# The front of an FNet-plus-MLP kernel: 128-column warm products, ScalarE centering part of the fourth chunk, first products ahead of the last transposes, and w1's second chunk in 4 loads

## The chip, the cores and the metric

The kernel runs on 1 core of one Trainium2 chip. The metric is the device time of one execution in microseconds, lower is better. Before the change it is 851.08 us, the median of 3 runs from 850.71 to 851.48.

## The reference: what is computed

x is 2048 rows (S) by 640 columns (D). It is normalized by row, and two branches read the result: a Fourier mixing along both dimensions of which the real part is kept, and a two-layer MLP with F = 1536. All inputs and the output are f32.

```python
xn = _layernorm(x, axis=-1)
a = einsum("bsd,ed->bse", xn, dft_hid_re)
b = einsum("bsd,ed->bse", xn, dft_hid_im)
y = einsum("ts,bse->bte", dft_seq_re, a) - einsum("ts,bse->bte", dft_seq_im, b)
h = gelu(einsum("bsd,df->bsf", xn, w1) + b1)
out = x + y + einsum("bsf,fd->bsd", h, w2) + b2
```

## The kernel before

**Products in pairs.** Every f32 operand of a large product is split into two fp32r tiles: ScalarE copies it to fp32r (the high part, L160 in `split`), VectorE subtracts that from the source (the low part, L161). A product of two such operands is three matmuls into one bank: high by high, high by low, low by high (L278 to L280, and L304 for the first layer of the MLP). Each matmul has a 128x128 stationary and a 128x512 moving operand.

**The MLP's first token block.** The tokens come in 4 blocks of 512. The first block stands at the front of the program and is the only part that the change touches. Its 512 rows are 4 chunks of 128 rows (x0 to x3, `xt`). `hidden(g)` makes the hidden values of unit g, that is of 128 columns of w1: 5 pieces j of D by 3 matmuls, 15 in all, into one bank. `hidden(0)` takes its 15 in the order of the list FIRST, pairs (j, kind) with kind 0 = high by high, 1 = high w1 by low x, 2 = low w1 by high x. `hidden(1)` takes kind 2 last. The first block's row scale 1/sqrt(var + eps) is not in the operands: it is multiplied in later, so the first products need centered rows only.

**The front, engine by engine.** The order of the instructions is written out by hand; every engine works its own list in that order and waits where an operand is missing.

- SyncE starts the loads of x0, x2, then w1's first unit in 8 loads (a first part of two pieces j, a second of three, each over 4 quarters), its second unit in 8, its third in 4, then w2 rows and a bias. ScalarE's queue starts x1 and x3.
- VectorE clears `zeros`, copies it as fp32r into `as` (L665, L667), takes the mean of x0 (L185, L186), centers x0 (L705, `center`), does the same for x2, centers x3 in two parts (pieces 0 and 1, then 2 to 4), and subtracts for the low parts of w1's first unit in two parts (L729).
- ScalarE takes the sums of x1 and x3 (L699, `sum_on_act`), centers x1 (L716), makes the high parts of w1's first unit in two parts (L728), and then the high parts of the five pieces of the transposed x (L160).
- TensorE runs NWARM = 10 products of the cleared tile (L676, `warm_up`; nothing reads their result), transposes the 5 pieces of x0 and of x1 into five banks `tacc` (L693, `transpose_x`), runs one more warm product, transposes x2 and x3 (pieces 0 and 1 of both, then 2 to 4 of both), and goes on to `hidden(0)` and `hidden(1)` (L304, 30 matmuls), a first one of `hidden(2)`, 4 transposes that spread the row scale (L764), and the rest. Piece j of the transposed x can be split when all four chunks have written bank `tacc[j]`.

After that, VectorE and ScalarE prepare one unit of w1 and w2 while TensorE multiplies another, to the end of the block.

Of the kernel before, what the change touches and what calls it, by code (L numbers as in the profile page):

```python
# [12 lines left out]
AF = mybir.ActivationFunctionType  # L13
ALU = mybir.AluOpType

P = 128
Q = 4
B = 32
EPS = 1e-5
NWARM = 10  # L20
TAIL = 4
ASIDE = 1
PADL = 8
# [3 lines left out]
def kernel(  # L27
# [38 lines left out]
    nc = tc.nc  # L66
    x = x.flatten_outer_dims()
    out = out.flatten_outer_dims()
    S, D = x.shape
    F = w1.shape[1]  # L70
    TB = 512
# [3 lines left out]
    ND = D // P  # L75
# [30 lines left out]
    def bank(k):  # L106
        return banks[:, k]
# [7 lines left out]
    MV = const.tile([P, 4, 6], F32, name="mv")  # L115
# [25 lines left out]
    slots, whole = {}, {}  # L141
# [8 lines left out]
    def chunked(ap):  # L150

        return ap.rearrange("p (c q i) -> p q c i", q=Q, i=B)

    def split(hi, lo, src, perm=False):

        h, l, s = (hi, lo, src)
        if perm:
            h, l = chunked(hi), chunked(lo)
            s = src.rearrange("p (q c i) -> p q c i", q=Q, i=B)
        nc.scalar.activation(h, s, AF.Copy)  # L160
        nc.vector.tensor_tensor(l, s, h.bitcast(F32), op=ALU.subtract)  # L161
# [12 lines left out]
    xt = {}  # L174
# [5 lines left out]
    def ln_stats(c):  # L180
        m = MV
        st = ST[c % 2]
        half = D // 2
        for h in range(2):
            nc.vector.bn_stats(st[:, h, :], xt[c][:, h * half : (h + 1) * half])  # L185
        nc.vector.bn_aggr(m[:, c % 4, 0:2], st.rearrange("p a b -> p (a b)"))  # L186
# [31 lines left out]
    XT, zt = {}, {}  # L218
# [27 lines left out]
    W1, W2, w1r, w2r = {}, {}, {}, {}  # L246

    def load_w1(i, eng=nc.sync, cuts=(0, ND)):
        if i >= NF:
            return  # L250
        t = early.tile([P, ND, P], F32, tag="w1r", bufs=3, name=f"w1r{i}")
        w1r[i] = t
        v = w1.rearrange("(q c i) f -> q i c f", q=Q, i=B)
        for c0, c1 in zip(cuts, cuts[1:]):
            for q in range(Q):
                eng.dma_start(t[q * B : (q + 1) * B, c0:c1], v[q, :, c0:c1, i * P : (i + 1) * P])

    def load_w2(i, eng=nc.sync):
        if i >= NF:
            return  # L260
        t = early.tile([P, D], F32, tag="w2r", bufs=3, name=f"w2r{i}")
        w2r[i] = t
        eng.dma_start(t, w2[i * P : (i + 1) * P, :])

    def prep_w1(i):
        if i < NF:
            W1[i] = slots[1, i]
            split(W1[i][:, 0], W1[i][:, 1], w1r.pop(i).rearrange("p a b -> p (a b)"))
# [18 lines left out]
    def unit(g):  # L287
        return g if g < NF else LATE[g % NF]

    def hidden(g, aside=None):  # L290
        i = unit(g)
        acc = bank(g % 3)
        kinds = ((0, 0), (0, 1), (1, 0))
        steps = [(j, k) for j in range(ND) for k in range(3)]
        if g == 0:
            steps = FIRST
        if g == 1:

            steps.sort(key=lambda s: s[1] == 2)
        for n, (j, k) in enumerate(steps):  # L300
            if aside and n == ASIDE:
                aside()
            a, b = kinds[k]
            nc.tensor.matmul(  # L304
                acc, W1[i][:, a, j * P : (j + 1) * P], XT[j][:, b], start=n == 0, stop=n == len(steps) - 1
            )
        return acc


    FIRST = [(0, 0), (0, 2), (1, 0), (1, 2), (0, 1), (2, 0), (2, 2), (1, 1), (3, 0), (3, 2)]  # L310
    FIRST += [(2, 1), (4, 0), (4, 2), (3, 1), (4, 1)]

    def gelu(g, acc, fill=lambda k: None):

# [338 lines left out]
    zeros = rows.tile([P, TB], F32, tag="yt", bufs=2, name="zeros")  # L653
# [8 lines left out]
            slots[key] = t[:, k * 2 * D : (k + 1) * 2 * D].rearrange("p (a b) -> p a b", a=2)  # L662
    nc.gpsimd.memset(eps, EPS)
    make_identity(nc, ident)
    nc.vector.memset(zeros, 0.0)  # L665
    warm = whole["as"][:, :TB]
    nc.vector.tensor_copy(warm, zeros)  # L667

    nc.scalar.activation(eps[:, 1:2], eps[:, 0:1], AF.Sqrt)
    load_w1(0, cuts=(0, 2, ND))  # L670
    load_w1(1, cuts=(0, 2, ND))

    wacc = bank(0)

    def warm_up():
        nc.tensor.matmul(wacc, warm[:, :P], warm, start=True, stop=True)  # L676

    for k in range(NWARM):
        warm_up()
    load_w1(2)  # L680
    load_w2(0)
    nc.sync.dma_start(b1c, b1.rearrange("(i p) -> p i", p=P))
    load_w2(1)
# [3 lines left out]
    tacc = [bank(3 + j) for j in range(ND)]  # L687

    xp = out_pool.tile([P, NC, D], F32, tag="zo", bufs=1, name="xp")

    def transpose_x(c, j0, j1):
        for j in range(j0, j1):
            nc.tensor.transpose(tacc[j][:, c * P : (c + 1) * P], xp[:, c, j * P : (j + 1) * P], ident)  # L693
# [4 lines left out]
    def sum_on_act(c):  # L698
        nc.scalar.activation(scratch, xt[c], AF.Copy, scale=-1.0 / D, accum_out=MV[:, c, 5:6])  # L699
# [4 lines left out]
    def center(c, op, shift, j0=0, j1=ND):  # L704
        nc.vector.tensor_scalar(  # L705
            chunked(xp[:, c])[:, :, j0:j1],
            xt[c].rearrange("p (q c i) -> p q c i", q=Q, i=B)[:, :, j0:j1],
            shift,
            None,
            op0=op,  # L710
        )
# [7 lines left out]
    ln_stats(0)  # L719
    center(0, ALU.subtract, MV[:, 0, 0:1])  # L720
    ln_stats(2)
    center(2, ALU.subtract, MV[:, 2, 0:1])
    sum_on_act(3)
    center(3, ALU.add, MV[:, 3, 5:6], 0, 2)
    center(3, ALU.add, MV[:, 3, 5:6], 2, ND)
    for lo, hi in ((0, 2 * P), (2 * P, D)):
        h, l = (W1[0][:, k, lo:hi] for k in range(2))
        nc.scalar.activation(h, first_w1[:, lo:hi], AF.Copy)  # L728
        nc.vector.tensor_tensor(l, first_w1[:, lo:hi], h.bitcast(F32), op=ALU.subtract)  # L729
    transpose_x(0, 0, ND)  # L730
    transpose_x(1, 0, ND)
    warm_up()
    for j0, j1 in ((0, 2), (2, ND)):
        transpose_x(2, j0, j1)
        transpose_x(3, j0, j1)
    for j in range(ND):
        split(XT[j][:, 0], XT[j][:, 1], tacc[j])
    load_w1(3)
    load_w1(4)
    for q in range(Q):  # L740
        nc.sync.dma_start(b2c[q * B : (q + 1) * B], b2[q * DQ : (q + 1) * DQ].rearrange("(c i) -> i c", i=B))
    acc0 = hidden(0)
    prep_w1(1)
    acc1 = hidden(1)

    nc.gpsimd.tensor_scalar(MV[:, 1::2, 0], MV[:, 1::2, 5], -1.0, None, op0=ALU.mult)
    square_on_act(1)
# [14 lines left out]
    def spread():  # L762
        for c in range(NC):
            nc.tensor.transpose(bank(7)[:, c * P : (c + 1) * P], wide[:, c * P : (c + 1) * P], ident)  # L764

    acc2 = hidden(2, spread)
    nc.vector.tensor_tensor(AB[:, 0], AB[:, 0], bank(7), op=ALU.mult)
    gelu(0, acc0)
# [282 lines left out]
    for g in range(NG):  # L1051
        t, i = divmod(g, NF)
# [95 lines left out]
    for q in range(1, NF // 2):  # L1148
        p = q - 1
# [100 lines left out]
    for n in range(1, 2 * NF):  # L1250
        blk, i = divmod(n, NF)
# [484 lines left out]
    for kind, what in stages:  # L1736
        b = blocks.index(what) if kind == "s" else b
# [63 lines left out]
```

## Time and profile before

| | |
|---|---|
| median of 3 runs | 851.08 us (850.71 to 851.48) |
| the profiled execution's own time | 850.46 us |
| its span, first to last instruction | 848.7 us |
| TensorE busy | 841.7 us, 99% of the span |
| VectorE, ScalarE busy | 666.8 us (79%), 356.0 us (42%) |
| first warm product | at 1.91 us |
| first transpose | at 6.42 us |
| first product of the MLP | at 9.66 us |

A timeline row gives the start from the span's beginning, the time from the first start to the last end of the rows merged in it, the engine (PE = TensorE, PEld = its weight loads, DVE = VectorE, ACT = ScalarE, SPq = SyncE's DMA queue), the line of the kernel, operation, out<-in, shapes, the count, and in brackets how long the engine had been idle and what ended that. Consecutive matmuls overlap in these rows: a record is longer than the step from one to the next.

### The profile page before, as it was taken

The page shows a single profiled execution, that of the slowest core. Times are in us where ns is not written, and L with a number is a line of the kernel's source. Part 1 is how long each engine was busy: PE and PEld are TensorE (multiplying, and loading weights), DVE is VectorE, ACT ScalarE, POOL GpSimd, SP SyncE. Part 2 cuts the span into 40 slices and gives each one's busy share as a digit, 9 for nine tenths or more (in the row PEclk, how much of TensorE's full clock was granted, in tenths as well). Part 3 has the DMA queues.
Part 4 walks back from the last instruction along what each step waited for, and adds up shares of the span by engine and source line. Part 5 has one row for each costly group of instructions (what it writes and reads, how often), then busy time and mean ns, then how long its engine had stood idle before and what let it go on. Part 6 is the DMA issues. An engine that isn't in the chain of part 4 may idle for free.

```text
span 848.7 us, 10340 instructions
## 1 busy us (share of the span) xinstructions
PE 841.7 (99%) x3707; PEld 695.2 (82%) x3707; DVE 666.8 (79%) x841; ACT 356.0 (42%) x499; POOL 48.9 (6%) x70
## 2 busy tenths in 40 slices
PE   9999999999999999999999999999999999999997
PEld 7888888878888888888888888888888888888886
DVE  6665766776758888779988887889967898885687
ACT  7454534456665555343444344232323433223241
POOL 0000311031221400000000000000000000000001
PEclk9999999999999999999999999999999999999999
DMA  6667699837679989858644679663865779705464
GB/s 182 192 184 188 159 228 252 193 87 189 202 245 355 358 186 174 173 132 188 152 137 111 162 229 289 151 150 98 205 168 169 253 191 229 306 19 180 124 172 108
DMA packets 207491, 158.45 MB, mean 187 GB/s; under 512 B 81040, under 2 KB 180880, under 8 KB 206928
## 3 DMA queue, kind: packets, MB, share of 16 engines
q1 hardware_dynamic: 198752, 135.25, 62.7%
q0 software_dynamic: 4144, 21.24, 6.3%
q10 hardware_dynamic: 4544, 1.31, 0.6%
q8 instruction: 29, 0.48, 0.3%
q14 instruction: 22, 0.18, 0.1%
HBM read 114.76 MB, written 42.99 MB: 186 GB/s over the span
## 4 chain that ended last, share of the span: by engine, by line
PE 99%; DVE 0%; issue 0%
PE banks L278 29%; PE banks L279 29%; PE banks L280 29%; PE banks L304 10%; PE banks L676 1%; PE banks L693 0%; PE banks L336 0%; PE banks L339 0%; PE banks L337 0%; DVE yo L1766 0%; DVE zeros L665 0%; DVE as L667 0%; PE banks L764 0%
## 5 line engine op out<-in xcount | busy, mean ns | idle before, releaser
L278 PE MATMUL banks<-as,xab 128*128 128x512 f32 x411 | 159.9, 389 | 0.0
L280 PE MATMUL banks<-as,xab 128*128 128x512 f32 x411 | 159.9, 389 | 0.0
L279 PE MATMUL banks<-as,xab 128*128 128x512 f32 x411 | 159.9, 389 | 0.0
L160 ACT ACTIVATE as<-r 128x1024 fp32r<-128x1024 f32 x80 | 85.0, 1062 | 178.1 <-PE banks L280 149.7
L161 DVE TENSOR_TENSOR as<-r,as 128x1024 fp32r<-128x1024 f32 x80 | 97.2, 1216 | 41.5 <-ACT as L160 41.5
L278 PEld LDWEIGHTS banks<-as,xab 128*128 128x128 f32 x411 | 77.1, 188 | 16.1
L279 PEld LDWEIGHTS banks<-as,xab 128*128 128x128 f32 x411 | 77.1, 188 | 16.0
L280 PEld LDWEIGHTS banks<-as,xab 128*128 128x128 f32 x411 | 77.1, 188 | 16.0
L278 PE MATMUL banks<-as,xc 128*128 128x512 f32 x224 | 87.1, 389 | 0.0
L279 PE MATMUL banks<-as,xc 128*128 128x512 f32 x224 | 87.1, 389 | 0.0
L280 PE MATMUL banks<-as,xc 128*128 128x512 f32 x224 | 87.1, 389 | 0.0
L160 ACT ACTIVATE as<-rt 128x1024 fp32r<-128x1024 f32 x32 | 34.0, 1062 | 70.5 <-PE banks L280 62.5
L304 PE MATMUL banks<-xtt,xab 128*128 128x512 f32 x240 | 57.1, 391 | 0.0
L304 PEld LDWEIGHTS banks<-xtt,xab 128*128 128x128 f32 x240 | 44.7, 188 | 9.8 <-ACT xtt L160 0.4
L278 PEld LDWEIGHTS banks<-as,xc 128*128 128x128 f32 x224 | 42.0, 188 | 8.8
L279 PEld LDWEIGHTS banks<-as,xc 128*128 128x128 f32 x224 | 42.0, 188 | 8.7
L280 PEld LDWEIGHTS banks<-as,xc 128*128 128x128 f32 x224 | 42.0, 188 | 8.7
L161 DVE TENSOR_TENSOR as<-rt,as 128x1024 fp32r<-128x1024 f32 x32 | 38.8, 1211 | 5.3 <-ACT as L160 5.3
L160 ACT ACTIVATE as<-u 128x1024 fp32r<-128x1024 f32 (+1 forms) x24 | 22.1, 920 | 48.2 <-PE banks L280 48.2
L512 DVE STREAM_TRANSPOSE r<-raw 128x1024 f32<-128x1024 f32 x32 | 39.5, 1240 | 3.1 <-PE banks L280 2.6
L161 DVE TENSOR_TENSOR as<-u,as 128x1024 fp32r<-128x1024 f32 (+1 forms) x24 | 24.9, 1042 | 18.8 <-ACT as L160 18.8
L512 DVE STREAM_TRANSPOSE rt<-raw 128x1024 f32<-128x1024 f32 x32 | 38.8, 1230 | 0.9 <-PE banks L280 0.8
(352 smaller groups left out, 1618.5 us busy)
## 6 DMA issues: line engine op xcount, KB each, us to landing
raw<-in_A_dft_seq_re_dram SPq DMA_DIRECT2D x64, 256.0 KB, 5.6
raw<-in_A_dft_seq_im_dram SPq DMA_DIRECT2D x64, 256.0 KB, 5.0
ws<-wit SPq DMA_DIRECT2D x15, 384.0 KB, 5.4
xs<-x SPq DMA_DIRECT2D x64, 80.0 KB, 1.8
xo<-in_A_x_dram SPq DMA_DIRECT2D x16, 320.0 KB, 6.7
xab<-wit SPq DMA_DIRECT2D x13, 384.0 KB, 4.2
wit<-wstp POOLq DMA_DIRECT2D x12, 384.0 KB, 3.7
x<-in_A_x_dram SPq DMA_DIRECT2D x14, 320.0 KB, 4.4
```

The lines of the kernel that those rows point to most:

```text
L160: nc.scalar.activation(h, s, AF.Copy)
L161: nc.vector.tensor_tensor(l, s, h.bitcast(F32), op=ALU.subtract)
L278: nc.tensor.matmul(acc, wh, mh, start=first, stop=False, skip_group_check=goes_on)
L279: nc.tensor.matmul(acc, wh, ml, start=False, stop=False, skip_group_check=goes_on)
L280: nc.tensor.matmul(acc, wl, mh, start=False, stop=last, skip_group_check=goes_on)
L304: nc.tensor.matmul(acc, W1[i][:, a, j * P : (j + 1) * P], XT[j][:, b], start=n == 0, stop=n == len(steps) - 1)
L512: nc.vector.transpose(held(pieces[g][2], u).rearrange("p c (n i) -> p c n i", i=B), r.rearrange("p n (c i) -> p c n i", i=B))
L676: nc.tensor.matmul(wacc, warm[:, :P], warm, start=True, stop=True)
```

## The change

Five edits, all in the front:

1. **Warm products.** They read `zeros` itself, as plain f32, 128x128 by 128x128, instead of fp32r 128x128 by 128x512. VectorE clears 128 columns instead of 512, and the copy into `as` is gone. NWARM goes from 10 to 13.
2. **Centering.** x3's pieces 0 and 1 are centered on ScalarE. VectorE centers x2 in two parts, and x3's pieces 2 to 4 after the first low part of w1.
3. **Order of splits.** The second part of w1's first unit is split after the first two pieces of x instead of ahead of all five.
4. **Order on TensorE.** x2 and x3 are transposed piece 0 of both, then x3's piece 1, then x2's pieces 1 to 4; two products of `hidden(0)` come before the last three transposes, those of x3's pieces 2 to 4. The 30 products of the first two units become one list (`first_two`) in which three of `hidden(1)` stand ahead of the last two of `hidden(0)`, and FIRST changes in its order.
5. **Loads.** w1's second unit comes in 4 loads, its third in 8. The 20 loads together stay 20.

```diff
-NWARM = 10
+NWARM = 13
...
+    def first_two():
+
+        kinds = ((0, 0), (0, 1), (1, 0))
+        second = sorted(((j, k) for j in range(ND) for k in range(3)), key=lambda s: s[1])
+        order = [(0, s) for s in FIRST[:13]] + [(1, s) for s in second[:2]]
+        order += [(0, FIRST[13]), (1, second[2]), (0, FIRST[14])] + [(1, s) for s in second[3:]]
+        for n, (g, (j, k)) in enumerate(order):
+            if n == 2:
+                transpose_x(3, 2, ND)
+                for e in range(2, ND):
+                    split(XT[e][:, 0], XT[e][:, 1], tacc[e])
+                prep_w1(1)
+            a, b = kinds[k]
+            ends = FIRST if g == 0 else second
+            nc.tensor.matmul(
+                bank(g),
+                W1[g][:, a, j * P : (j + 1) * P],
+                XT[j][:, b],
+                start=(j, k) == ends[0],
+                stop=(j, k) == ends[-1],
+            )
+        return bank(0), bank(1)
...
-    FIRST = [(0, 0), (0, 2), (1, 0), (1, 2), (0, 1), (2, 0), (2, 2), (1, 1), (3, 0), (3, 2)]
-    FIRST += [(2, 1), (4, 0), (4, 2), (3, 1), (4, 1)]
+    FIRST = [(0, 0), (0, 2), (1, 0), (1, 2), (0, 1), (2, 0), (1, 1), (3, 0), (2, 2), (3, 2)]
+    FIRST += [(4, 0), (4, 2), (2, 1), (3, 1), (4, 1)]
...
-    nc.vector.memset(zeros, 0.0)
-    warm = whole["as"][:, :TB]
-    nc.vector.tensor_copy(warm, zeros)
+    nc.vector.memset(zeros[:, :P], 0.0)
...
-    load_w1(1, cuts=(0, 2, ND))
+    load_w1(1)
...
-        nc.tensor.matmul(wacc, warm[:, :P], warm, start=True, stop=True)
+        nc.tensor.matmul(wacc[:, :P], zeros[:, :P], zeros[:, :P], start=True, stop=True)
...
-    load_w1(2)
+    load_w1(2, cuts=(0, 2, ND))
...
-    center(2, ALU.subtract, MV[:, 2, 0:1])
     sum_on_act(3)
-    center(3, ALU.add, MV[:, 3, 5:6], 0, 2)
-    center(3, ALU.add, MV[:, 3, 5:6], 2, ND)
-    for lo, hi in ((0, 2 * P), (2 * P, D)):
+
+    def split_first(lo, hi):
         h, l = (W1[0][:, k, lo:hi] for k in range(2))
         nc.scalar.activation(h, first_w1[:, lo:hi], AF.Copy)
         nc.vector.tensor_tensor(l, first_w1[:, lo:hi], h.bitcast(F32), op=ALU.subtract)
+
+    nc.scalar.activation(
+        chunked(xp[:, 3])[:, :, :2],
+        xt[3].rearrange("p (q c i) -> p q c i", q=Q, i=B)[:, :, :2],
+        AF.Identity,
+        bias=MV[:, 3, 5:6],
+    )
+    center(2, ALU.subtract, MV[:, 2, 0:1], 0, 2)
+    center(2, ALU.subtract, MV[:, 2, 0:1], 2, ND)
+    split_first(0, 2 * P)
+    center(3, ALU.add, MV[:, 3, 5:6], 2, ND)
     transpose_x(0, 0, ND)
     transpose_x(1, 0, ND)
     warm_up()
-    for j0, j1 in ((0, 2), (2, ND)):
-        transpose_x(2, j0, j1)
-        transpose_x(3, j0, j1)
-    for j in range(ND):
+    transpose_x(2, 0, 1)
+    transpose_x(3, 0, 2)
+    transpose_x(2, 1, ND)
+    for j in range(2):
         split(XT[j][:, 0], XT[j][:, 1], tacc[j])
+    split_first(2 * P, D)
...
-    acc0 = hidden(0)
-    prep_w1(1)
-    acc1 = hidden(1)
+    acc0, acc1 = first_two()
```

What this makes of three engines' lists at the front is shown below; the number behind a name tells buffers apart.

TensorE from the first warm product to the row-scale transposes of the third unit, before (`as` and `zeros` are the cleared tiles, `ident,xp` a transpose of centered rows, `xtt,xab` a product of the transposed x with w1, xab_122 for units 0 and 1, xab_123 for unit 2):

```order
L676 MATMUL banks<-as 128x512 x10
L693 MATMUL banks<-ident,xp 128x128 x10
L676 MATMUL banks<-as 128x512
L693 MATMUL banks<-ident,xp 128x128 x10
L304 MATMUL banks<-xtt,xab_122 128x512 x30
L304 MATMUL banks<-xtt,xab_123 128x512
L764 MATMUL banks<-ident,ab 128x128 x4
```

The same stretch of TensorE's list in the changed kernel:

```order
L692 MATMUL banks<-zeros 128x128 x13
L709 MATMUL banks<-ident,xp 128x128 x10
L692 MATMUL banks<-zeros 128x128
L709 MATMUL banks<-ident,xp 128x128 x7
L304 MATMUL banks<-xtt,xab_122 128x512 x2
L709 MATMUL banks<-ident,xp 128x128 x3
L304 MATMUL banks<-xtt,xab_122 128x512 x28
L322 MATMUL banks<-xtt,xab_123 128x512
L788 MATMUL banks<-ident,ab 128x128 x4
```

Three transposes moved behind the first two products, and the 11 warm products became 14 of another shape.

ScalarE from the sum of x3 (x_120) to the high part of w1's second unit, before (w1r_139 is the first unit as loaded, w1r_148 the second):

```order
L699 ACTIVATE ab,mv<-x_120 128x640
L728 ACTIVATE xab_122<-w1r_139 128x256
L728 ACTIVATE xab_122<-w1r_139 128x384
L160 ACTIVATE xtt<-banks 128x512 x5
L160 ACTIVATE xab_122<-w1r_148 128x640
```

The same stretch of ScalarE's list in the changed kernel (w1r_138 the first unit, w1r_147 the second):

```order
L715 ACTIVATE ab,mv<-x_120 128x640
L745 ACTIVATE xp<-x_120,mv 128x4x2x32
L742 ACTIVATE xab_122<-w1r_138 128x256
L160 ACTIVATE xtt<-banks 128x512 x2
L742 ACTIVATE xab_122<-w1r_138 128x384
L160 ACTIVATE xtt<-banks 128x512 x3
L160 ACTIVATE xab_122<-w1r_147 128x640
```

One centering of 256 columns came in, and w1's second part (384 columns) moved behind two of the five pieces of x.

VectorE from the aggregate of x2's statistics (x_118 is x2, x_120 is x3) to the low part of w1's second unit, before:

```order
L186 BN_AGGR mv<-st_89 128x2
L705 TENSOR_SCALAR xp<-x_118,mv 128x4x5x32
L705 TENSOR_SCALAR xp<-x_120,mv 128x4x2x32
L705 TENSOR_SCALAR xp<-x_120,mv 128x4x3x32
L729 TENSOR_TENSOR xab_122<-w1r_139,xab_122 128x256
L729 TENSOR_TENSOR xab_122<-w1r_139,xab_122 128x384
L161 TENSOR_TENSOR xtt<-banks,xtt 128x512 x5
L161 TENSOR_TENSOR xab_122<-w1r_148,xab_122 128x640
```

The same stretch of VectorE's list in the changed kernel:

```order
L186 BN_AGGR mv<-st_89 128x2
L721 TENSOR_SCALAR xp<-x_118,mv 128x4x2x32
L721 TENSOR_SCALAR xp<-x_118,mv 128x4x3x32
L743 TENSOR_TENSOR xab_122<-w1r_138,xab_122 128x256
L721 TENSOR_SCALAR xp<-x_120,mv 128x4x3x32
L161 TENSOR_TENSOR xtt<-banks,xtt 128x512 x2
L743 TENSOR_TENSOR xab_122<-w1r_138,xab_122 128x384
L161 TENSOR_TENSOR xtt<-banks,xtt 128x512 x3
L161 TENSOR_TENSOR xab_122<-w1r_147,xab_122 128x640
```

The centering of x3's first two pieces left VectorE, that of its last three moved behind w1's first low part, and w1's second low part moved behind two low parts of x.

More of the change, by code (lines that the diff above doesn't have):

```diff
@@ L294, in hidden @@
         steps = [(j, k) for j in range(ND) for k in range(3)]
[L295 to L299, printed above, removed]
         for n, (j, k) in enumerate(steps):
```

## The prediction

> **What bounds the kernel now.** I read the page first, for which engine sets the end.
>
> ```profile
> span 848.7 us, 10340 instructions
> ...
> PE 841.7 (99%) x3707; PEld 695.2 (82%) x3707; DVE 666.8 (79%) x841; ACT 356.0 (42%) x499; POOL 48.9 (6%) x70
> ...
> PE 99%; DVE 0%; issue 0%
> ```
>
> TensorE is busy 99% and the chain of work that ended last is TensorE's. The busy time per stretch says from where on it has no gap at all.
>
> ```profile
> 24.00:100.00 76.00, 76.00 (x337) 62.89 (x336) 52.87 (x101) 40.67 (x61) 2.09 (x2) 1.00 0.70 183
> ...
> 700.00:840.00 140.00, 140.00 (x620) 115.86 (x618) 110.95 (x109) 44.38 (x45) 2.65 (x4) 1.00 0.56 165
> ```
>
> From 24 us on every stretch is filled (76.00 of 76.00, 140.00 of 140.00). So what the front saves or loses ahead of the main stream reaches the end one for one, and nothing else can. The front is read from TensorE's timeline.
>
> ```profile
> 1.91 4.63 PE L676 MATMUL banks<-as 128*128 128x512 f32 x10 [1.91 <-DVE as L667]
> 6.42 1.98 PE L693 MATMUL banks<-ident,xp 128*128 128x128 f32 x10
> 8.16 0.48 PE L676 MATMUL banks<-as 128*128 128x512 f32 x1
> 8.48 1.25 PE L693 MATMUL banks<-ident,xp 128*128 128x128 f32 x10
> 9.66 7.46 PE L304 MATMUL banks<-xtt,xab 128*128 128x512 f32 x31
> 16.96 0.60 PE L764 MATMUL banks<-ident,ab 128*128 128x128 f32 x4
> 20.59 0.39 PE L336 MATMUL banks<-hs,rt 128*128 128x512 f32 x1
> 22.86 1.30 PE L339 MATMUL banks<-hs,rt 128*128 128x512 f32 x5
> ```
>
> Useful products start at 9.66. TensorE is "busy" before, but with warm products that nobody reads. Steps follow from these rows, first start to last start: a product takes (1.30 - 0.39) / 4 = 0.227. The 31st product starts at 9.66 + 7.46 - 0.39 = 16.73, 7.07 after the first, where 30 steps are 6.82: 0.25 is lost in waits. Where, the weight loads say.
>
> ```profile
> 9.65 0.30 PEld L304 LDWEIGHTS banks<-xtt,xab 128*128 128x128 f32 x2 [0.16 <-ACT xtt L160]
> ...
> 13.21 0.53 PEld L304 LDWEIGHTS banks<-xtt,xab 128*128 128x128 f32 x3 [0.25 <-ACT xab L160]
> ```
>
> One wait is for the transposed x, one at 13.21 for w1's second unit. Early transposes are slower than late ones: the pieces of TensorE's timeline below give a step of (1.30 - 0.42) / 4 = 0.22 for the first five, against (1.25 - 0.27) / 9 = 0.11 for the second ten above, and a warm product costs 4.63 - 4.21 = 0.42.
>
> ```profile
> 1.91 4.21 PE L676 MATMUL banks<-as 128*128 128x512 f32 x9 [1.91 <-DVE as L667]
> ...
> 6.42 1.30 PE L693 MATMUL banks<-ident,xp 128*128 128x128 f32 x5
> ...
> L693 PE MATMUL banks<-ident,xp x5: 421/421/447, 6.4 to 7.3; 128*128 128x128 f32 x5
> ...
> L693 PE MATMUL banks<-ident,xp x15: 271/273/421, 7.5 to 9.5; 128*128 128x128 f32 x15
> ```
>
> A transpose falls from 421 to 273 ns soon after 7.5, so TensorE's clock stepped up at about 7.6, 5.7 after the first warm product.
>
> Behind the first product stands ScalarE, and behind it VectorE and a load.
>
> ```profile
> 1.43 0.43 DVE L667 CAST as<-zeros 128x512 fp32r<-128x512 f32 x1
> 5.72 0.56 DVE L705 TENSOR_SCALAR xp<-x,mv 128x640 f32<-128x640 f32 x1
> 7.14 0.21 DVE L186 BATCH_NORM_AGGREGATE mv<-st 128x2 f32<-128x12 f32 x1
> 7.38 1.15 DVE L705 TENSOR_SCALAR xp<-x,mv 128x640 f32<-128x640 f32 x3
> 8.44 0.42 DVE L729 TENSOR_TENSOR xab<-w1r,xab 128x256 fp32r<-128x256 f32 x1
> 9.63 3.08 DVE L161 TENSOR_TENSOR xtt<-banks,xtt 128x512 fp32r<-128x512 f32 x5
> ...
> 6.56 0.74 ACT L699 ACTIVATE ab<-x 128x640 f32<-128x640 f32 x1 [0.15 <-DMA x<-in_A_x_dram]
> 7.20 0.19 ACT L699 ACTIVATION_READ_ACCUMULATOR ab<-x 128x1 f32 x1
> 7.30 0.40 ACT L728 ACTIVATE xab<-w1r 128x256 fp32r<-128x256 f32 x1
> 8.47 0.53 ACT L728 ACTIVATE xab<-w1r 128x384 fp32r<-128x384 f32 x1 [0.77 <-DMA w1r<-in_B_w_dram]
> 9.01 2.56 ACT L160 ACTIVATE xtt<-banks 128x512 fp32r<-128x512 f32 x5
> 12.42 0.74 ACT L160 ACTIVATE xab<-w1r 128x640 fp32r<-128x640 f32 x1 [0.86 <-DMA w1r<-in_B_w_dram]
> 16.09 0.62 ACT L755 ACTIVATE ab<-mv 128x512 f32<-128x512 f32 x1
> 19.58 0.63 ACT L326 ACTIVATE hs<-ab 128x512 fp32r<-128x512 f32 x1
> ```
>
> ScalarE's first split of x starts at 9.01, right behind w1's second part, which waited 0.77 for its load. TensorE's transposes allow hardly more: bank 0 needs the fourth of the last ten, 8.48 + 3 x 0.11 + 0.27, about 9.0 (piece 0 of x3 is third: 8.97). Two chains thus end there together, and both must go for a gain.
>
> **The change part by part, late end first.** *Warm products.* The copy (0.43) leaves VectorE and the clear shrinks to a quarter, so TensorE starts 0.5 to 0.9 sooner; I take 1.2. A plain f32 product of 128 columns is in no row. Below it lies one pass of a quarter of the present 512 columns, 0.42 / 4 = 0.11; above, four transposes of the same shape, 4 x 0.22 = 0.88. I take 0.42, four quarters: the kernel itself needs three fp32r products (L278 to L280) for one f32 product, so one pass cannot do, and four with their weight loads hidden are the row they replace. The Trainium skill, "FP8 and Floating Point Precision", TensorE Precision Notes, gives true f32 four passes through the array, which would be 0.42; no row here shows it. 13 x 0.42 = 5.5 then end at 6.7 if the clock stays low.
>
> *First transposes.* They need VectorE's centering, 5.72 + 0.56 = 6.28; they start at 6.42 now, at 6.7 then. At the same lag of 5.7 the clock rises at 6.9, so ten cost 1.3 instead of 1.74 (6.42 to 8.16) and end at 8.0. The single warm product there costs 0.2, as the present one, so x2's first transpose starts near 8.25, x3's piece 0 is done at 8.25 + 0.11 + 0.27 = 8.65.
>
> *Centering and splits.* ScalarE adds a 256-column centering behind 7.20 + 0.19; the nearest row is 0.40 (L728), so it ends at 7.85, w1's first part at 8.2. VectorE no longer holds x3's pieces 0 and 1. The half centering of x2 is ready at about 7.75. So x's first split starts at 8.65 instead of 9.01, with the load of w1's second part no longer ahead of it, and the first product at 9.66 - 0.36 = 9.3.
>
> *The three transposes* that stood ahead of the first product now stand behind two: 3 x 0.11 = 0.33 given back. VectorE's centering for them comes behind L729 (0.42), ending near 9.0, covered.
>
> *Feeding the 30.* ScalarE puts 0.53 (w1's second part) between piece 1 and piece 2 of x, whose steps are 0.49 (2.56 in five). Piece 2 is ready 0.60 + 0.49 + 0.53 + 0.49 = 2.1 at most after the first split's start, i.e. about 1.45 after the first product; the list asks for it as its sixth, 5 x 0.227 + 0.33 = 1.47 after. It just fits; the rest have 0.2 and more. w1's second unit is asked for last of all: its load in four pieces goes out earlier.
>
> ```profile
> 6.57 2.31 SPq L256 DMA_DIRECT2D w1r<-in_B_w_dram  x5
> ...
> w1r<-in_B_w_dram SPq DMA_DIRECT2D x4, 80.0 KB, 2.0
> ```
>
> Its four starts now end at 8.88, and 80 KB loads land in 2.0, so by 10.9 instead of before 12.42: the wait at 13.21 goes. I count the 0.25 of waits as gained. SyncE's list keeps 20 loads, so the third unit lands when it did, and all behind it.
>
> *Sum, late end:* 0.36 + 0.25 - 0.33 = 0.3 (0.2 if the fit above fails once).
>
> *Early end.* If the clock is up by 6.4, the products end before 6.28, the first ten transposes take 1.1 from 6.42, and x3's piece 0 waits for ScalarE's centering, 7.85: bank 0 is full at 8.2, when ScalarE is free too. The split starts at 8.2 instead of 9.01, the sum is 0.8 + 0.25 - 0.33 = 0.72. The Trainium skill, "TensorE: Matmul & The Clock Gate", Part 1, says that the clock rises after one busy window of about 3.4 us, and that the window is free-running. By that rule the step comes between 3.4 and 6.8 after the first product, this trace's 5.7 agrees, and a start at 1.2 would rise anywhere from 4.6 to 8.0, so runs would spread over both ends.
>
> Behind that nothing is tight: the row scale (16.09 + 0.62 = 16.71, against the transposes at 16.96) moves earlier with w1's second unit (0.86 of waiting gone), and the gelu's high part, 19.58 + 0.63 = 20.21, has 0.4 to the products at 20.59 and moves with it.
>
> I take the middle, 0.5: 850.46 becomes 849.96 for the profiled execution, whose own time lies 0.6 under the median of 851.08; against that median **850.6**.
>
> **The rivals.** *Dear warm products (slower).* TensorE works in order, so the transposes wait for all 13. If one costs four transposes, 0.88, they end at 1.2 + 11.4 = 12.6 with a low clock, 6.2 after 6.42; with a step up at 6.9 the last six and a half halve, ending at 9.8, 3.4 late. Less the 0.5: +2.9 to +5.7, 854.0 to 856.8. It decides from (6.9 - 1.2) / 13 = 0.44 at a low clock, where the gain is used up soon after. For it: the transpose, the only row of this shape and type, steps at twice a quarter of the wide product. Against: in the wide product the weight load (PEld) overlaps, so the doubling may be the transpose's own.
>
> *Warm products too light.* At 0.11 to 0.22 the 13 end by 2.6 to 4.1, TensorE idles until 6.42 and the clock stays low. All transposes step at 0.22: the first product comes at about 9.9, 0.2 late, and until 6.42 + 5.7 = 12.1 products take 0.42 instead of 0.227, losing half of 2.2; with the three transposes +1.4, 852.5 (852.0 to 853.2).
>
> *The gain is eaten.* ScalarE carries 0.40 more ahead of the first split, and w1's second part now splits x's pieces; with a warm product at 0.5 or a miss at every fit, 0.3 to 0.5 goes again: 851.1. For it: the sixth product fits by 0.02.
>
> **How the numbers follow.** Forecast 0.61 (849.9 to 851.3 with the runs' spread), gain eaten 0.14, dear 0.14, too light 0.08, a larger gain than all this 0.03. 0.2% of 851.08 is 1.7 us, about what a measurement of this kernel can tell from no change: faster means below 849.4, slower above 852.8. Slower gets the dear case and half of the light one, 0.18; faster 0.03; within 0.79. The range reaches from 849.9 to 853.0: it leaves out the dear case and the larger gain, 0.17.
>
> **What would show it.** Right: the first warm product near 1.2, the 13 over by 6.7, transposes from 6.4 to 6.7, x's first split between 8.2 and 8.7, the first product between 8.9 and 9.3, no wait of the weight loads for w1's second unit, row-scale transposes 0.3 to 0.7 before 16.96. Wrong: a transpose that starts after 7, or products of 600 ns behind 10 us. If the first product comes sooner and the row-scale transposes don't, the feeding ate it.

## The result, and the profile after

The changed kernel takes 853.11 us (median of 16 runs, 850.73 to 854.00); the kernel before takes 850.83 in 16 runs on the same chip (850.30 to 851.70). The ratio is 1.0023, with a 95% interval of 1.0017 to 1.0030. That is slower by 2.3 us, where 850.6 was forecast with a range up to 853.0. Three of the 16 runs lie at 850.7 to 851.5 and the others between 852.1 and 854.0. The profiled execution took 853.09.

The page of the changed kernel, span, busy times and chain:

```profile
span 851.3 us, 10373 instructions
...
PE 843.2 (99%) x3724; PEld 697.1 (82%) x3724; DVE 665.7 (78%) x840; ACT 356.1 (42%) x500; POOL 48.8 (6%) x70
...
PE 84%; DVE 4%; DMA 4%; issue 3%; ACT 2%; SPq 2%; POOL 0%; DVEq 0%; ACTq 0%; POOLq 0%
```

TensorE still reads 99%, but the chain that ended last is TensorE's for only 84% of the span (99% before): somewhere it leaves TensorE and runs through loads and VectorE. TensorE has 17 weight loads and 17 matmuls more (3724 against 3707).

The front gained less than was forecast, but lost nothing. TensorE's timeline of the changed kernel:

```profile
1.04 5.92 PE L692 MATMUL banks<-zeros 128*128 128x128 f32 x26 [1.04 <-DVE zeros L683]
6.75 1.42 PE L709 MATMUL banks<-ident,xp 128*128 128x128 f32 x10
...
8.23 0.93 PE L709 MATMUL banks<-ident,xp 128*128 128x128 f32 x7
9.30 0.73 PE L304 MATMUL banks<-xtt,xab 128*128 128x512 f32 x2
9.87 0.49 PE L709 MATMUL banks<-ident,xp 128*128 128x128 f32 x3
...
16.66 0.39 PE L322 MATMUL banks<-xtt,xab 128*128 128x512 f32 x1
16.89 0.60 PE L788 MATMUL banks<-ident,ab 128*128 128x128 f32 x4
```

The 13 warm products show as 26 matmuls, and 16.89 stands against 16.96 before: the front ends 0.07 early, not late. So the 2.6 us that the span grew by were lost later. The waits of the changed kernel between 125 and 185 us (engine and line, what it waited for, us in all, times, longest) say where:

```profile
ACT banks L881 <- DVE ab L389: 2.6, 1, 2.6
PEld banks L278 <- ACT banks L881: 2.0, 1, 2.0
PE banks L278 <- ACT banks L881: 1.6, 1, 1.6
```

The same rows of the kernel before, which has none for TensorE itself:

```profile
ACT banks L857 <- DVE ab L371: 2.4, 1, 2.4
PEld banks L278 <- ACT banks L857: 0.3, 1, 0.3
```

ScalarE waits for VectorE in both kernels. New is that TensorE and its weight loads have to wait behind it.

TensorE's timeline of the changed kernel at that place:

```profile
180.45 0.39 PE L280 MATMUL banks<-xc,xab 128*128 128x512 f32 x1
182.42 0.50 PE L278 MATMUL banks<-xtt,tw 128*128 128x512 f32 x1 [1.58 <-ACT banks L881]
```

The step from 180.45 to 182.42 is 1.97 where products step by 0.227: 1.74 lost. With the smaller waits at 136.7 (0.48), 144.0 (0.11) and 157.6 (0.31) that is 2.64. Aligned product by product, the changed kernel is 0.05 ahead until 136 us, 2.6 behind from 182.4 on, and stays there. The chain of waits leads back from 182.42 (start, duration, engine and what it made):

```profile
71.41 8.53 DMA z<-xs
80.06 0.71 DVE zt L238
...
113.53 3.05 DMA wraw<-in_A_dft_hid_im_dram
...
147.62 7.52 DMA wit<-wst
...
181.06 0.64 DVE ab L389
181.78 0.59 ACT banks L881
```

It begins at z, the normalized rows of the second token block, loaded from where the kernel stored them (xs), and goes by VectorE's list, SyncE's list, the Fourier weights (wraw, wit) and the bank copy to TensorE. The rows of z in the changed kernel: its four loads and VectorE's transposes of it (durations in ns, least, median and most; first and last start in us) and the time from issue to landing:

```profile
L234 SPq DMA_DIRECT2D z<-xs x4: 316/485/492, 70.0 to 71.4; - x4
L238 DVE STREAM_TRANSPOSE zt<-z x3: 704/712/712, 80.1 to 84.7; 128x512 f32<-128x512 f32 x3
DMA to landing us min/median/max: 3.9/5.4/8.5
```

The same rows of the kernel before:

```profile
L234 SPq DMA_DIRECT2D z<-xs x4: 315/485/489, 70.1 to 71.5; - x4
L238 DVE STREAM_TRANSPOSE zt<-z x4: 704/711/712, 78.6 to 84.6; 128x512 f32<-128x512 f32 x4
DMA to landing us min/median/max: 4.0/5.6/7.0
```

The loads go out at the same time (70.0 to 71.4 against 70.1 to 71.5), but the last quarter takes 8.5 instead of 7.0 and lands at 79.9 instead of 78.5. What lay beside it, the DMA queues tell. First the changed kernel's instruction queue from 76.0 to 77.6 us (packets, MB, share of 16 engines):

```profile
q8 instruction: 1, 0.02, 5.2%
```

Then the kernel before, which has no such packet in that window but one from 80.0 to 81.4:

```profile
q8 instruction: 1, 0.02, 4.5%
```

One packet of 16 KB of instructions holds one DMA engine for 5.2% of 16 x 1.6 us, 1.33 us. In the trace it starts at 76.28 in the changed kernel, while z's last pieces are under way, and at 80.46 before, when z has landed. The page counts 29 such packets; (3707 + 3707) / 29 is 256 weight loads and matmuls each, which fits TensorE's own program, one packet about every 29 us; the runs below move them by changing TensorE's instructions alone. The Trainium skill, "Runtime: NRT & Kernel Launch", Instruction fetch mechanics, says that each engine's sequencer fetches its program by its own DMA queue in blocks of 16 KiB, 256 instructions, and calls the cost mostly hidden. The size and count agree with this trace; hidden it is here from TensorE, which does not stop at 76.28, but not from the load beside it.

### The profile page after: what moved, and what is told of

It is laid out like the page before. It is cut to its first block, busy times and chain, and to the rows that moved or that the text cites. A ratio compares the mean times of both kernels' runs of the same rounds, so it can differ in the third digit from the quotient of the medians.

```text
span 851.3 us, 10373 instructions
## 1 busy us (share of the span) xinstructions
PE 843.2 (99%) x3724; PEld 697.1 (82%) x3724; DVE 665.7 (78%) x840; ACT 356.1 (42%) x500; POOL 48.8 (6%) x70
## 4 chain that ended last, share of the span: by engine, by line
PE 84%; DVE 4%; DMA 4%; issue 3%; ACT 2%; SPq 2%; POOL 0%; DVEq 0%; ACTq 0%; POOLq 0%
PE banks L278 27%; PE banks L279 27%; PE banks L280 26%; PE banks L322 2%; DMA wit<-wst 2%; DMA z<-xs 1%; SPq L406 1%; PE banks L304 1%; PE banks L692 1%; SPq L203 0%; ACT ab L340 0%; DVE xtt L161 0%; DVE zt L238 0%; DVE st L185 0%; DMA wraw<-in_A_dft_hid_im_dram 0%
## 5 line engine op out<-in xcount | busy, mean ns | idle before, releaser
L322 PE MATMUL banks<-xtt,xab 128*128 128x512 f32 x210 | 50.0, 390 | 0.0
L322 PEld LDWEIGHTS banks<-xtt,xab 128*128 128x128 f32 x210 | 39.4, 188 | 8.1
```

The costliest lines, as they stand in the source:

```text
L322: nc.tensor.matmul(acc, W1[i][:, a, j * P : (j + 1) * P], XT[j][:, b], start=n == 0, stop=n == len(steps) - 1)
```

## The experiments

**Theory** ("code loading" in the expectations). The 17 added weight-load and matmul pairs use up TensorE's program sooner, which moves the third instruction load from 80.5 to 76.3, onto z; z then lands too late for slack that ends at 182 us. **Rivals:** other parts of the change (the order at the front, the four loads of w1) cost it ("early front"); plain f32 products cost something later ("plain f32"); or more instructions cost time as such ("more instructions"). Each run below stands beside the kernel before on the same chip (median 850.46, 850.52 and 850.52 in the three groups).

### Fewer pairs, the rest of the change kept: six warm products of 256 columns

```diff
-NWARM = 13
+NWARM = 6
-    nc.vector.memset(zeros[:, :P], 0.0)
+    nc.vector.memset(zeros[:, :256], 0.0)
-        nc.tensor.matmul(wacc[:, :P], zeros[:, :P], zeros[:, :P], start=True, stop=True)
+        nc.tensor.matmul(wacc[:, :w], zeros[:, :P], zeros[:, :w], start=True, stop=True)
-        warm_up()
+        warm_up(256)
```

Here w is 256 for the six and 128 for the one in the middle: 3 pairs more than before instead of 17.

> The changed kernel with its 13 first warm products of 128 columns replaced by 6 of 256, still plain f32 from the same cleared tile. Each plain f32 product shows as two weight loads and two matmuls, so TensorE's list has 3 pairs more than before the change instead of 17. Theory code loading: TensorE's third load of 16 KB of instructions moves back from 76.3 us to near 79.7, off the last packets of the z load; the z transposes start near 78.6, TensorE has no gap at 136 to 182 us, and the time is 850.2 to 850.9. Theory early front (the new order at the front shifts the loads and engines behind it): the front is the same, so the time stays at 853. Theory plain f32 (that kind of product costs something later): stays at 853.

850.20 (849.96 to 851.07), ratio 0.9997 (0.9988 to 1.0006). TensorE's timeline (first products, row-scale transposes), then z's rows:

```profile
8.79 0.73 PE L304 MATMUL banks<-xtt,xab 128*128 128x512 f32 x2
...
16.41 0.60 PE L788 MATMUL banks<-ident,ab 128*128 128x128 f32 x4
```

```profile
L234 SPq DMA_DIRECT2D z<-xs x4: 316/485/489, 69.5 to 70.9; - x4
...
DMA to landing us min/median/max: 3.7/5.3/6.7
```

The instruction load comes at 79.2, z lands at 70.9 + 6.7 = 77.6, and TensorE has no gap behind the front. The loss of 2.3 us is gone with everything but the warm products' shape and number kept. These products are plain f32 too, so that kind of product is not what costs.

### The warm products undone, the rest kept

```diff
-NWARM = 13
+NWARM = 10
-    nc.vector.memset(zeros[:, :P], 0.0)
+    nc.vector.memset(zeros, 0.0)
+    warm = whole["as"][:, :TB]
+    nc.vector.tensor_copy(warm, zeros)
-        nc.tensor.matmul(wacc[:, :P], zeros[:, :P], zeros[:, :P], start=True, stop=True)
+        nc.tensor.matmul(wacc, warm[:, :P], warm, start=True, stop=True)
```

> The changed kernel with the first edit alone undone: 10 fp32r products of 512 columns from the copied tile, all other edits kept; as many pairs on TensorE as before. Theory code loading: third instruction load near 80.5 us less what the front gains, no gap at 136 to 182 us, 850.2 to 850.9, which is also what the other four edits are worth. Theory early front: near 853. Theory plain f32: as code loading, 850.2 to 850.9.

850.39 (849.92 to 850.90), ratio 0.9998 (0.9989 to 1.0007). The instruction load is at 80.0, z lands at 78.1, there is no gap, and the row-scale transposes start at 16.67. The reordering and the four loads cost nothing that shows.

### The warm products alone, in the kernel before

```diff
-NWARM = 10
+NWARM = 13
-    nc.vector.memset(zeros, 0.0)
-    warm = whole["as"][:, :TB]
-    nc.vector.tensor_copy(warm, zeros)
+    nc.vector.memset(zeros[:, :P], 0.0)
-        nc.tensor.matmul(wacc, warm[:, :P], warm, start=True, stop=True)
+        nc.tensor.matmul(wacc[:, :P], zeros[:, :P], zeros[:, :P], start=True, stop=True)
```

> The kernel before with the first edit alone: 13 plain f32 warm products of 128 columns from the cleared tile, everything else as before the change. 17 pairs more on TensorE than before. Theory code loading: the third instruction load falls near 76.3 us, the z load lands 1.4 us late, the time is 852.5 to 853.7. Theory early front: the front's new order is not there, so 850.5 to 851.0. Theory plain f32: 853.

851.58 (850.36 to 853.35), ratio 1.0015 (1.0007 to 1.0024). z's rows, and TensorE's waits between 125 and 185 us:

```profile
L234 SPq DMA_DIRECT2D z<-xs x4: 315/485/489, 69.9 to 71.3; - x4
...
DMA to landing us min/median/max: 4.0/5.6/8.1
```

```profile
PE banks L278 <- ACT banks L855: 1.1, 1, 1.1
```

The load comes at 77.0, z lands at 71.3 + 8.1 = 79.4, and the same gap stands at 180.8 with 1.23 us. So this one edit makes a loss at the same place by itself, but 1.1 of the 2.3 us in the median, less than was expected; its load came 0.75 later than in the full change and z landed 0.5 earlier.

### Both: six of 256 columns in the kernel before

```diff
-NWARM = 10
+NWARM = 6
-    nc.vector.memset(zeros, 0.0)
-    warm = whole["as"][:, :TB]
-    nc.vector.tensor_copy(warm, zeros)
+    nc.vector.memset(zeros[:, :256], 0.0)
-        nc.tensor.matmul(wacc, warm[:, :P], warm, start=True, stop=True)
+        nc.tensor.matmul(wacc[:, :w], zeros[:, :P], zeros[:, :w], start=True, stop=True)
-        warm_up()
+        warm_up(256)
```

> The kernel before with 6 plain f32 warm products of 256 columns and one of 128: 3 pairs more than before. Theory code loading: 850.6 to 851.1, as before. Theory early front: the same. Theory plain f32: 853.

850.44 (850.17 to 851.33), ratio 1.0001 (0.9993 to 1.0010). The load is at 79.75, z lands at 78.1, no gap. The row-scale transposes start at 16.92 (16.96 before), so the earlier warm-up bought nothing in this execution; with 13 products of 128 columns, in the run above, they start at 16.69.

### Nine warm products of 192 columns: nine pairs more

```diff
-NWARM = 13
+NWARM = 9
-        warm_up()
+        warm_up(192)
```

The clear is 192 columns wide too.

> The changed kernel with 9 first warm products of 192 columns: 9 weight-load and matmul pairs more than before the change on TensorE, between the 3 and the 17 of the kernels seen. At 0.227 a pair the third instruction load falls near 78.2 us, after the last packets of the z load (77.5 to 77.7). Theory code loading: z lands by 78.5, 850.2 to 851.0. Theory more instructions (the cost grows with the pairs, half way between 3 and 17): about 851.6.

850.87 (850.07 to 854.32), ratio 1.0005 (0.9995 to 1.0014). In the profiled execution, which took 850.45, the load came at 79.1, z landed at 78.2, and there is no gap at 136 to 182.

### Still more pairs: eight and eighteen tiny products

The tiny ones are 32 x 32 and stand ahead of ten of 128 columns, 27 and 47 pairs more than before. Eight of them:

```diff
-NWARM = 13
+NWARM = 10
+    for k in range(8):
+        nc.tensor.matmul(wacc[:B, :B], zeros[:, :B], zeros[:, :B], start=True, stop=True)
```

> The changed kernel with 8 plain f32 warm products of 32 by 32 ahead of 10 of 128 by 128: 27 pairs more than before the change. The third instruction load falls near 74.0 us, in the middle of the z load's packets. Theory code loading: the DMA engine that takes it is late with its share, z lands about as late as in the changed kernel, 852 to 854. Theory more instructions: above 854.

851.82 (850.62 to 853.55), ratio 1.0012 (1.0004 to 1.0021). The load's moment was missed: it came at 71.2, where z's loads are being issued. One issue took 2.0 us, so the last quarter goes out at 73.0 instead of 71.4:

```profile
L234 SPq DMA_DIRECT2D z<-xs x4: 316/486/2026, 70.0 to 73.0; - x4
```

z lands at 79.8, and the gap at 181.1 is 1.38. Eighteen of them:

```diff
-NWARM = 13
+NWARM = 10
+    for k in range(18):
+        nc.tensor.matmul(wacc[:B, :B], zeros[:, :B], zeros[:, :B], start=True, stop=True)
```

> The changed kernel with 18 tiny products ahead of 10 of 128 by 128: 47 pairs more than before the change, the most of all. The third instruction load falls near 69.5 us, before the z load's packets begin (70.7). Theory code loading: z lands by 78.6 again, no gap in TensorE at 136 to 182 us from this, 850.2 to 851.2 (0.3 of it for a later first transpose). Theory more instructions: 855 and more. Theory early front: 853 as in the changed kernel.

852.48 (851.60 to 853.92), ratio 1.0022 (1.0013 to 1.0031). A miss: the load was to clear z and did not. z's rows:

```profile
L234 SPq DMA_DIRECT2D z<-xs x4: 316/485/489, 71.8 to 73.2; - x4
```

The load came at 67.1, on the stores to xs that z is loaded from: z went out at 71.8 instead of 70.0 and landed at 80.1. Some 0.6 of this is TensorE's own stream, which ran 0.64 late there (row-scale transposes at 17.28, 0.32 late). The theory needs widening: the sensitive place seems to be the whole passage from xs's stores to z's landing, about 67 to 78 us. For the stores this rests on this one run. The rival "more instructions cost more" falls too, since 17 pairs cost 2.3, 27 cost 1.3 and 47 cost 2.0 us.

### The 17 pairs kept, z made earlier

Half of the 16 stores to xs just ahead of the z load go out by GpSimd's queue instead of SyncE's; the front and its warm products are those of the change.

```diff
-    def ln_apply(c, eng=nc.vector):
+    def ln_apply(c, eng=nc.vector, store=nc.sync):
-            nc.sync.dma_start(xs[c % NC * NC + k, c // NC * B : (c // NC + 1) * B], xt[c][k * B : (k + 1) * B])
+            store.dma_start(xs[c % NC * NC + k, c // NC * B : (c // NC + 1) * B], xt[c][k * B : (k + 1) * B])
-                ln_apply(c)
+                ln_apply(c, store=nc.gpsimd if c < 6 else nc.sync)
```

> The changed kernel with all its warm products, 17 pairs more than before, but 8 of the 16 stores ahead of the z load started from GpSimd's queue instead of SyncE's, so the z load can start 1 to 2 us sooner. Theory code loading: the instruction load at 76.3 then meets the x loads behind z instead of z's last packets; z lands before 78, the loss at 136 to 182 us falls by more than half: 850.5 to 852. Theory early front or plain f32: 853. If the stores from GpSimd land later than thought, z starts no sooner and the run tells nothing.

850.26 (850.08 to 852.78), ratio 0.9999 (0.9990 to 1.0007). The queues from 77.4 to 79.0, then z's rows:

```profile
q8 instruction: 1, 0.02, 4.1%
```

```profile
L234 SPq DMA_DIRECT2D z<-xs x4: 316/485/500, 69.2 to 70.7; - x4
...
DMA to landing us min/median/max: 3.7/5.4/6.8
```

The load still comes early, at 77.55, but z goes out 0.75 earlier, lands at 77.5 just before it, and there is no gap at 136 to 182. With the pairs kept and z out of the way, the 2.3 us come back in the median. That separates the instruction load's meeting with z from the pairs themselves. The profiled execution took 851.08; it loses 0.4 at 205 to 210 us and 0.5 at 670 us, away from this gap.

### Both remedies

```diff
-        warm_up()
+        warm_up(256)
-                ln_apply(c)
+                ln_apply(c, store=nc.gpsimd if c < 6 else nc.sync)
```

These are the edits of the first experiment and of the one above, together.

> The changed kernel with 6 warm products of 256 columns (3 pairs more than before instead of 17) and with 8 of the stores ahead of the z load on GpSimd's queue: the third instruction load near 79.5 us and the z load about 0.8 us sooner are both clear of each other. Theory code loading: no loss behind the front, what the front gains stays, 850.0 to 850.4 and no run above 851.5. If something else than the meeting of the two loads costs time behind the front, above 850.5.

850.07 (849.95 to 850.65), ratio 0.9997 (0.9988 to 1.0005), load at 79.5, z landed at 77.7. It cannot be told from the kernel before.

### Four light warm products

```diff
-NWARM = 13
+NWARM = 4
```

> The changed kernel with 4 warm products instead of 13: they end near 2.8 us, 1 pair less than before the change, so the instruction loads lie as before it. If the prediction's rival of too light warm products has its mechanism right, the clock is still low when the transposes start at 6.4 and steps up only near 10 to 12 us; transposes step by 0.22, the first product comes at 9.9 or later and the first products step by 0.42: 851.4 to 853. If the clock does not need the 13, 850.2 to 850.5.

852.01 (851.77 to 852.63), ratio 1.0019 (1.0010 to 1.0028). TensorE's timeline, the first ten transposes and the row-scale transposes:

```profile
6.60 2.37 PE L709 MATMUL banks<-ident,xp 128*128 128x128 f32 x10 [3.48 <-DVE xp L721]
...
18.21 0.49 PE L788 MATMUL banks<-ident,ab 128*128 128x128 f32 x3
```

The transposes step slowly, (2.37 - 0.42) / 9 = 0.22, and the row-scale transposes are 1.25 late. z lands at 79.8 here too, yet there is no gap at 136 to 182: TensorE itself is as late.

### The loads of w1's second unit in two parts again

On the kernel with six warm products of 256 columns (850.20):

```diff
-    load_w1(1)
+    load_w1(1, cuts=(0, 2, ND))
-    load_w1(2, cuts=(0, 2, ND))
+    load_w1(2)
```

> The changed kernel with 6 warm products of 256 columns and w1's second unit in 8 loads, its third in 4, as before the change. The prediction counted the wait for w1's second unit, 0.25, as gained by the loads. If so, a wait of the weight loads on ScalarE's split of w1's second unit comes back near 13 us and the row-scale transposes start 0.2 to 0.6 later than with 4 loads (16.41), 850.3 to 850.7. If the second unit is asked for late enough anyway, nothing changes, 850.2.

850.95 (850.72 to 851.32), ratio 1.0005 (0.9997 to 1.0014). TensorE's timeline, products and row-scale transposes:

```profile
13.01 4.16 PE L304 MATMUL banks<-xtt,xab 128*128 128x512 f32 x17 [0.45 <-ACT xab L160]
...
17.24 0.60 PE L788 MATMUL banks<-ident,ab 128*128 128x128 f32 x4
```

The wait for the second unit is back at 13.01 and grown. 17.24 against 16.41 is 0.83 in the front, of which 0.10 lies ahead of the first product (8.89 against 8.79); the medians differ by 0.75 to 0.9 (850.20 in another group, 850.04 in the same one for the next kernel).

### The three transposes ahead of the first two products again

On the same kernel:

```diff
-            if n == 2:
+            if n == 0:
```

> The changed kernel with 6 warm products of 256 columns and the last three transposes ahead of the first two products again. The prediction let the first product start without them and counted 0.33 as given back behind it. If right, the two cancel but for the wait on ScalarE: the first product at the same time (TensorE waits there for ScalarE's first split), the row-scale transposes 0.0 to 0.35 earlier than 16.41. If the transposes do hold the first product up, the first product comes 0.1 to 0.3 later and nothing is won behind it. Time 849.9 to 850.4 in either case.

850.04 (849.90 to 850.98), ratio 0.9996 (0.9988 to 1.0005). TensorE's timeline, with the thirty products and the row-scale transposes:

```profile
9.18 7.11 PE L304 MATMUL banks<-xtt,xab 128*128 128x512 f32 x30
...
16.36 0.60 PE L788 MATMUL banks<-ident,ab 128*128 128x128 f32 x4
```

The first product starts 0.39 later than in the first experiment (9.18 against 8.79) and the row-scale transposes at 16.36 against 16.41: the order makes no difference.

## Why the prediction was right and wrong

**The warm products' price held.** The 26 matmuls take 5.92, so a pair steps by (5.92 - 0.42) / 25 = 0.22 and a product, which is two pairs, costs 0.44; 0.42 was taken. TensorE started at 1.04 and the 13 ended at 7.0 (1.2 and 6.7 were forecast). The dear case, 0.88, fell. The Trainium skill's four passes for true f32 ("FP8 and Floating Point Precision", TensorE Precision Notes) agree: an estimate of 0.11 for one pass, a quarter of the old product's 0.42, makes 0.44.

**The first product came at 9.30**, the figure of the late end. Which end comes differs from execution to execution. The run with z made earlier has the same front, since its edit lies behind it, and its timeline reads:

```profile
6.54 1.25 PE L709 MATMUL banks<-ident,xp 128*128 128x128 f32 x10
...
8.92 0.73 PE L304 MATMUL banks<-xtt,xab 128*128 128x512 f32 x2
...
16.50 0.60 PE L788 MATMUL banks<-ident,ab 128*128 128x128 f32 x4
```

There the ten transposes take 1.25 instead of 1.42, so TensorE's clock had risen sooner, and the front ends 0.46 ahead of before instead of 0.07. The prediction had said that runs would spread over both ends. The 8.79 of the six wider products can't be put down to their shape for the same reason.

**The three transposes** were to give back the 0.33 that they won ahead of the first product. They did: moving them changed the first product by 0.39 and the row-scale transposes by 0.05.

**The feeding was mis-sized.** The prediction counted the 0.25 of waits as gained. Product by product, the kernel before lost only 0.10 of it at w1's second unit: the four products from 12.77 on take 1.17 - 0.39 = 0.78 for three steps, which are 0.68 without a wait. Another 0.11 lay between the first product and the second, and that step is as long in the changed kernel (0.73 - 0.39 = 0.34). From the first product to the 31st are 16.66 - 9.30 = 7.36, of which 30 x 0.227 = 6.82 and 0.33 for the transposes leave 0.21 of waits: this 0.11, and 0.10 in steps of a few hundredths up to the eleventh product. So the wait for w1's second unit went, and the fit of x's pieces, called just enough, all but held. Hence 0.36 + 0.25 - 0.33 - 0.21 = 0.07 in place of 0.3, the size of the rival "the gain is eaten", in this execution. With z made earlier (8.92, and the 31st at 16.27) the same sum is 0.74 + 0.25 - 0.33 - 0.20 = 0.46, about the 0.5 that was forecast. In medians, and leaving the four light products aside, the runs without the gap that keep the four loads lie between 0.48 us ahead of the kernel before and 0.35 behind it (nine of 192 columns), and their intervals all contain no change. The four loads were worth more than the wait that they removed: undoing them cost 0.73 behind the first product, because the second unit's products are asked for sooner while its load lands when it did.

(One slip had no effect: bank 0 needs the third of the last ten transposes, as the prediction's own 8.97 has it, not the fourth.)

**The light rival** was right in mechanism and size for four products: transposes at 0.22, 852.01 against the 852.5 named. It is not what happened, since 13 were heavy enough.

**The step that failed** is "reaches the end one for one, and nothing else can", with "Behind that nothing is tight". Both were read from TensorE's having no gap in the profile of before. That says that nothing was late there, not by how much it was early: z's last quarter landed at 78.5, less than 0.9 us ahead of where it costs. And the change's 17 added pairs were costed as time at the front only. They are also 34 instructions, which brought the later loads of TensorE's program forward, and the third one met z. Across the runs, with TensorE's own stream within 0.7 us of the one before: z landed by 78.5 in those without a gap at 182, and at 79.4, 79.8, 79.9 and 80.1 in those with one, of 1.23, 1.38, 1.74 and 1.74 us. No rival of mine held this mechanism. The time lies just beyond the range, and that it lies so close is luck: the high end came from the light case, which is another cause.

**What stays open.** How much of the 2.3 us a fourth instruction load adds is open. VectorE's delay of 1.4 us at z shrinks to 0.5 by 104 us and is 2.8 at 106, when the statistics of the next x start. In between the delay goes by SyncE's list. Its queue in the changed kernel:

```profile
96.43 7.29 SPq L203 DMA_DIRECT2D xs<-x  x16
...
105.72 6.12 SPq L406 DMA_DIRECT2D wraw<-in_A_dft_hid_re_dram  x4
111.93 2.10 SPq L406 DMA_DIRECT2D wraw<-in_A_dft_hid_im_dram  x4
```

The same rows of the kernel before:

```profile
95.00 7.36 SPq L203 DMA_DIRECT2D xs<-x  x16
...
104.77 4.32 SPq L388 DMA_DIRECT2D wraw<-in_A_dft_hid_re_dram  x4
109.19 2.84 SPq L388 DMA_DIRECT2D wraw<-in_A_dft_hid_im_dram  x4
```

The stores to xs start 1.43 late and the wraw loads 0.95 late, but the last wraw issue ends 2.00 late (114.03 against 112.03). The 1.05 more arises beside a fourth instruction load, which came at 106.04 and held its engine for 2.58 us (108.43 and 1.17 before). Such a meeting alone made no gap: with z made earlier the stores start at 95.02 and the fourth load came at 105.03, beside a first wraw issue of 2.0 us. What it adds to a late z was not tried apart. Each kernel was profiled once, so what sets its single executions apart (850.73 to 854.00 in the changed kernel) was not seen. And the gain at the front was not told from no change by any run.

## What to carry to other kernels

A kernel without gaps has slack that its profile doesn't show: before calling what lies behind an edit safe, look for the transfers that land last before their first use, and count what the edit adds to an engine's program, since the loads of that program share the DMA engines with the data. When a time moves without a wait at the edit, align both streams, find the first instruction that lags, and ask what lay beside its load. Of two warm-ups of about equal length, the one in fewer and wider products brought fewer instructions, and here that decided (850.20 against 853.11).

## What the runs showed that I had not expected

- A plain f32 product of 128 columns appears as two weight loads and two matmuls: 13 products as 26, at 0.44 us a product with the low clock; six of 256 columns show as 12, and one costs 0.88 (11 steps from 1.18 to 6.03, two a product).
- TensorE's program arrives in packets of 16 KB, 29 in the changed kernel, each holding one DMA engine for 0.9 to 2.6 us. A z piece that met one landed 1.4 us late.
- The packet's moment is not fixed by the count of instructions: with the same 17 pairs more it came at 76.3, 77.0 and 77.6 in three kernels, where 17 x 0.227 = 3.9 us ahead of 80.5 would be 76.6; with 27 and 47 more it came 9.3 and 13.3 ahead, where their number gives 6.1 and 10.7.
